# Float16 steps in pairs on TensorE, and the weights' float16 preparation at other slots

## The chip, the cores and the metric

One Trainium2 chip, one of its cores. The metric is the device time of one execution in microseconds, the median of several runs. A profile of a single execution, taken by the hardware profiler, stands beside the times.

## The reference

Two stages, in float32. First an attention through 32 inducing points, for 4 batches of 12416 rows of 128 values; then a gated feed-forward network (SwiGLU) over all 49664 rows.

```python
B, N, m, C = (4, 12416, 32, 128)          # x: (B, N, C), inducing: (m, C)
def mab(q, kv):
    s = scale * (q @ kv.transpose(0, 2, 1))
    s = s - s.max(-1, keepdims=True)
    a = np.exp(s)
    a /= a.sum(-1, keepdims=True) + 1e-09
    return a @ kv
h = mab(I, x)                             # 32 rows per batch
x = mab(x, h)                             # back to N rows
g = x @ w_gate                            # 128 -> 1536
silu = g * (1.0 / (1.0 + np.exp(-g)))
val = x @ w_val
return (silu * val) @ w_out               # 1536 -> 128
```

## The kernel before

The second attention is never multiplied out. Per batch, `tw` holds the 32 rows h projected through both weight matrices, and `stack` holds the attention weights of a tile of rows, transposed; one matmul of the two gives a 128 x 512 or 128 x 480 piece of g or of val. Both are split into a high and a low part so that float32r matmuls keep float32's accuracy.

A batch is 25 column tiles (`COLS`): one of 4 x 128 rows, twelve of 512, twelve of 480. A column tile has `NT` = 12 steps, t = 0 to 11, one for each 128 of the 1536 inner values. So a batch has 300 slots (`SLOTS`). In a slot, the main loop issues for one unit u:

- `front(u)`: two float32r matmuls on TensorE, g (line 787) and v (line 788), each into a buffer of the pool `ps_gv`, which has six.
- `gate(u)`: silu of g on ACT (line 793). It frees the g buffer.
- `value(u)`: the product of v and silu on DVE (line 801), into a buffer h, or, for t in `DVE_TILES` = {1, 5, 9} (`LAST_DVE` = {1, 7} in batch 3), in place in the v buffer.
- `split` of the unit before, which waited in the list `wait`: h_hi, the rounded product, by ACT (by DVE for t in `CAST`), line 814, and h_lo, the rest, by POOL, or by DVE for the units held in the v buffer, line 816. The unit then goes to the list `pend`.
- the attention's steps that are due at this slot, for this batch (`cur`) and the next (`nxt`).
- `back`: while `pend` and `wait` together hold more than `ahead` units, three matmuls of the oldest into o (lines 831, 832, 833: w_lo h_hi, w_hi h_hi, w_hi h_lo), in a buffer of the pool `ps_o`, which has two. After t = 11 DVE copies o to `ob` (line 841) and SP stores it.

From batch 0's column `CSW` = 13 on, and in all later batches, a unit is `half`: h_hi, h_lo and the weights of o are float16; g and v remain float32r. `ahead` is 5 (`SKEW`), grows by 1/6 a slot up to `HI` before a burst of exponentials (`bursts`, slots at which ACT computes the attention's exponentials), and falls back at it: TensorE then works off the stored units.

The schedule is manual: each engine executes its instructions in the order in which the program issues them, and waits only where data or a buffer require it. Steps of the attention carry a slot by hand (`plan`, `post`, `FIRST`). In batch 0 some more steps prepare float16: `peak_of` (nine reductions over the weights, line 190), `peak_a` and `peak_b` (their maximum over partitions through a matmul, line 198), `peak_c`, `peak_d`, the factors of h (`size_a` to `size_c`), `half_a` (w_hi + w_lo into `joint` on POOL, line 214), `half_b` and `half_c` (float16 weights, on ACT, line 218, and DVE, line 222), and `rise`, which scales val's part of `tw`. `acc` names the values of t at which a step that needs a `ps_o` buffer has to wait for a later slot.

Of the kernel before, what the change touches and what calls it, by code (L numbers as in the profile page):

```python
# [9 lines left out]
F32 = mybir.dt.float32  # L10
# [3 lines left out]
ALU = mybir.AluOpType  # L14
AX = mybir.AxisListType
# [4 lines left out]
P = 128  # L20
# [22 lines left out]
COLS = [(0, 0)] + [(q, j) for q in range(1, NF) for j in range(NG)]  # L43
SLOTS = len(COLS) * NT
NXT = 4
HI = 10
RAMP = 6
BF = (2, 3, 11, 10)
SKEW = 5
# [10 lines left out]
E0 = 36  # L60
TINY = 2.0 ** -50
LAST_DVE, LAST_CAST = {1, 7}, {5, 11}
WPK, WSZ, WOH, CSW = 104, 128, 134, 13

# [45 lines left out]
def induced_set_attention_then_swiglu(ctx: ExitStack, tc: tile.TileContext, xt, xn, ind, wgv, wo, out):  # L110
# [63 lines left out]
    nc.gpsimd.memset(wide, 2.0 ** 127)  # L174
    peak = const.tile([P, 12], F32, name="peak")
    top = const.tile([P, 36], F32, name="top")
    peaks = const.tile([P, P], F32, name="peaks")

    def floor2(out, in_):

        nc.vector.tensor_scalar(out=out.bitcast(U32), in0=in_.bitcast(U32), scalar1=0x7F800000, scalar2=None, op0=ALU.bitwise_and)
# [7 lines left out]
        at = 6 * k + i  # L189
        nc.vector.tensor_reduce(out=peak[:, at:at + 1], in_=w[:, WP * i:WP * i + WP], op=ALU.max, axis=AX.X, apply_absolute_value=True)  # L190

    def peak_a(k):
        nc.vector.tensor_reduce(out=peak[:, 10 + k:11 + k], in_=peak[:, (0, 6)[k]:(6, 9)[k]], op=ALU.max, axis=AX.X)
        nc.vector.tensor_scalar(out=peaks, in0=ones, scalar1=peak[:, 10 + k:11 + k], scalar2=None, op0=ALU.mult)

    def peak_b(k):
        ps = ps_gv.tile([P, 512], F32, name="gv")
        nc.tensor.matmul(out=ps[:, 0:P], lhsT=peaks, rhs=ident, start=True, stop=True)
        nc.vector.tensor_scalar(out=peaks, in0=ps[:, 0:P], scalar1=TINY, scalar2=None, op0=ALU.max, op1=ALU.max, accum_out=top[:, k:k + 1])

    def peak_c():
        floor2(top[:, 1:2], top[:, 1:2])
        inverse2(top[:, 2:3], top[:, 1:2])

# [65 lines left out]
    def attention(b, one, xn0=None, xt0=None):  # L270
# [180 lines left out]
            nc.vector.tensor_scalar(out=st.hV.bitcast(U32), in0=st.hT[:, 0:M].bitcast(U32), scalar1=0x7FFFFFFF, scalar2=None, op0=ALU.bitwise_and)  # L451

        def size_b():
            ps = ps_gv.tile([P, 512], F32, name="gv")
            nc.tensor.matmul(out=ps[:, 0:M], lhsT=ones, rhs=st.hV, start=True, stop=True)  # L455
            st.sc = att.tile([P, 8], F32, name="sc")
            c = lambda i: st.sc[:, i:i + 1]
            st.up, st.down = c(0), c(1)
            nc.vector.tensor_reduce(out=c(2), in_=ps[:, 0:M], op=ALU.max, axis=AX.X)
            nc.vector.tensor_scalar(out=c(3), in0=c(2), scalar1=top[:, 0:1], scalar2=TINY, op0=ALU.mult, op1=ALU.max)  # L460
            floor2(c(4), c(3))
            inverse2(c(5), c(4))
# [190 lines left out]
    def plan(st, p):  # L653

        f, s = st.f, []

        def add(slot, step, *args):
            def go():
                f[step](*args)


            go.acc = (NT - 1, 0, 1) + (2,) * (step == "hacc") if step in ("s1", "max_b", "hacc", "h_c", "s2") else ()
            s.append((slot, go))

        def blocks(q):
            return CH0[q], CH0[q] + CH[q]

        last = p["S1"][0] + p["S1"][1] * (NCH - 1)
        v1 = last - 3 * p["S1"][1]
        for q in range(NCH):  # L670
            add(p["LX"][0] + p["LX"][1] * q if q < NXT else v1 + 1 + 3 * (q - NXT), "load_xt", q)

            add(v1 if q < NXT else last, "s1", q, q not in (0, NXT))
        mb = last + p["MX"]
        add(last + 2, "max_a"), add(mb, "max_b")
        e1 = mb + p["E1"]
        for q in range(NXN):
            add(e1 - p["LN"][0] + p["LN"][1] * q, "load_xn", q)
            add(e1, "exp1_part", q)
            add(e1, "eT", q)  # L680
            add(e1 + p["HA"][q], "hacc", q, (0, NXN - 1))
        add(e1, "exp1_part", NXN, NCH - 1)
        for q in range(NXN, NCH):
            k = NXN + (q - NXN | 1)
            at = e1 + p["HB"][0] + p["HB"][1] * (k - NXN)
            add(max(at - p["HC"][0] - k + q, e1 + 1 + (p["HB"][0] + p["HB"][1] if q == NCH - 1 else p["HA"][0])), "load_xn", q)
            add(at - p["HC"][1] + 1 - k + q, "eT", q)
            add(at, "hacc", q, (k - 1, k))
        add(at, "h_a")
        add(at + 2, "h_b")  # L690
        hn = at + p["HD"]
        add(hn, "h_c")
        for i, step in enumerate(("size_a", "size_b", "size_c", "size_d")):
            add(hn + 3 * i + 2, step)
        for i, q in enumerate(S2O):
            k = i % NXT
            at = hn + 4 + p["H2"] * (NXT - 1) if i < NXT else hn + p["H2"] * (NCH - 1)
            add(at, "s2", *blocks(q), i not in (0, NXT))
# [162 lines left out]
    for b in range(B):  # L861
        nxt = attention(b + 1, (one, oneb)[(b + 1) % 2]) if b + 1 < B else None
        if nxt is not None:
            nxt.steps = plan(nxt, PA if b == 0 else PB)
            if b == 0:
                cur.steps.append((nxt.e1, lambda: run(f"e2:52:{NTB}")))
                for q in range(2, NF):
                    base = NT * (1 + NG * (q - 1) - NST) + 2
                    base = max(base, E0 + 4) if q < 4 else max(base, nxt.e1 + 1)
                    cur.steps += post(cur, q, nc.gpsimd, base)  # L870
                once = [lambda x=(k, i): peak_of(*x) for k in range(2) for i in range((6, 3)[k])]
                once += [lambda: cur.f["size_a"](), lambda: peak_a(0)]
                cur.steps += [(WPK + 2 * i, f) for i, f in enumerate(once)]
                once = [lambda: peak_b(0), lambda: peak_a(1), lambda: cur.f["size_b"](), lambda: peak_b(1), peak_c, peak_d, cur.f["size_c"]]
                cur.steps += [(WSZ + 2 * i, f) for i, f in enumerate(once)]
                cur.steps += [(WOH + 10 + 2 * i, lambda i=i: (half_a, half_b, half_c)[i // 3](i % 3)) for i in range(9)]
                cur.steps += [(NT * (CSW - 1) + 2 * i + 2, lambda i=i: cur.f["rise"](i)) for i in range(6)]
                cur.steps.sort(key=lambda x: x[0])
        bursts = (nxt.bursts if nxt is not None else set()) | ({E0} if b == 0 else set())
        last_burst = max(bursts, default=0)  # L880
        for slot in range(NT if b == 0 else 0, SLOTS):
            c, t = slot // NT, slot % NT
            u = front(cur, b, c, t)
            gate(u)
            value(u)
            u.cast_dve = t in (LAST_CAST if b == B - 1 else CAST)
            u.last = b == B - 1 and slot == SLOTS - 1
            if wait:
                split(wait[0])
                pend.append(wait.pop(0))  # L890
            wait.append(u)
            if slot in bursts:
                u.cast_dve = True
                split(u)
                pend.append(wait.pop(0))
            for a in (cur, nxt):
                while a is not None and a.steps and a.steps[0][0] <= slot:

                    if pend and pend[0].t in getattr(a.steps[0][1], "acc", ()):
                        break  # L900
                    a.steps.pop(0)[1]()
            ahead = min(ahead + 1 / RAMP, HI) if nxt is not None and slot < last_burst else max(ahead - 1 / RAMP, SKEW)
            if slot in bursts:
                ahead = SKEW - (b == 0)
            while len(pend) + len(wait) > ahead:
                back(pend.pop(0))
        if nxt is not None:
            nxt.steps = [(at - SLOTS, f) for at, f in nxt.steps]
        cur = nxt
# [41 lines left out]
```

## Time and profile before

| what | value |
|---|---|
| median of 3 runs | 1452.67 us (1452.27 to 1453.83) |
| the profiled execution | 1453.71 us |
| its span, first to last instruction | 1451.9 us |
| mean granted TensorE clock | 0.995 |
| busy share of the span | TensorE 99%, ACT 87%, DVE 83%, POOL 78% |
| batch 1's 300 slots | 349.5 us |
| batch 3, from its first slot | 331.2 us |

PE is TensorE's matmul, PEld its weight load, DVE VectorE, ACT ScalarE, POOL GpSimd, SP the engine that issues DMAs. A group's row gives line, engine, operation, output and inputs by the program's names, shapes and count, then busy us and mean ns of one, then idle time before it and who ended it. A timeline's row gives start and duration in us, then the same names, and in brackets the idle time before it with its releaser. A row of a stretch gives, for each engine, busy us and number of instructions, then the granted clock, the DMA engines' share and GB/s. The ends of matmuls are modelled and overlap, so it is their starts that tell the pace.

### The profile page before, as it was taken

Reading aid. Unit: us, or ns where it says so; the run is one execution under the profiler, and the core shown is the slowest. Engines: PE = TensorE matmul, PEld = TensorE weight load, DVE = VectorE, ACT = ScalarE, POOL = GpSimd, SP = SyncE. Lnnn points to the kernel's source line nnn. Section 1 sums busy time; section 2 is a strip of 40 time slices with the busy share of each in tenths; the row PEclk is TensorE's granted clock in tenths of the full one; section 3 lists DMA queues with packets and bytes.
Section 4 is the critical chain, followed back from the end, with each engine's and each line's share of the span. In section 5 each row is a group of like instructions: output and inputs, shape, how many; then the busy total and the mean of one; then the engine's idle time right before and its main releaser. Section 6 shows DMA issues by size and latency. Waiting matters only on the chain.

```text
span 1451.9 us, 25130 instructions
## 1 busy us (share of the span) xinstructions
PE 1434.0 (99%) x7512; PEld 825.1 (57%) x7512; DVE 1208.2 (83%) x2138; ACT 1266.5 (87%) x2366; POOL 1139.7 (78%) x1036
## 2 busy tenths in 40 slices
PE   9999998999999999999999999999999999999999
PEld 6577776555555555555555455455555555555554
DVE  6888878988888879888888878978888878888887
ACT  4889787789998788899999888799999898889897
POOL 1689768778788667787888767778878889889887
PEclk9999999999999999999999999999999999999999
DMA  9233522212132532121114324221111111111110
GB/s 373 63 98 119 180 87 85 96 52 76 32 111 76 185 129 106 52 70 41 42 36 144 129 88 137 106 74 49 39 42 43 32 42 45 31 44 39 41 42 21
DMA packets 50824, 119.82 MB, mean 83 GB/s; under 512 B 11392, under 2 KB 28288, under 8 KB 50688
## 3 DMA queue, kind: packets, MB, share of 16 engines
q1 hardware_dynamic: 50688, 118.22, 25.0%
q8 instruction: 59, 0.97, 0.3%
q14 instruction: 77, 0.63, 0.1%
HBM read 62.87 MB, written 25.43 MB: 61 GB/s over the span
## 4 chain that ended last, share of the span: by engine, by line
PE 81%; ACT 0%; DVE 0%; issue 0%; DVEq 0%
PE o L831 16%; PE gv L788 16%; PE gv L787 16%; PE o L833 15%; PE o L832 15%; PE gv L329 1%; PE o L377 1%; PE o L329 1%; PE gv L511 0%; ACT silu L793 0%; ACT h_hi L814 0%; DVE ob L841 0%; PE gv L390 0%; PE o L443 0%; PE gv L455 0%
## 5 line engine op out<-in xcount | busy, mean ns | idle before, releaser
L816 POOL TENSOR_TENSOR h_lo<-h,h_hi 128x480 f16<-128x480 f32 (+2 forms) x915 | 1035.4, 1153 | 262.8 <-ACT h_hi L814 185.3
L793 ACT ACTIVATE silu<-gv 128x512 f32<-128x512 f32 (+1 forms) x1200 | 702.8, 587 | 96.4 <-PE gv L787 73.5
L801 DVE TENSOR_TENSOR h<-gv,silu 128x512 f32<-128x512 f32 (+1 forms) x916 | 610.5, 668 | 185.0 <-ACT silu L793 126.3
L787 PE MATMUL gv<-stack,tw 128*128 128x512 f32 (+1 forms) x1200 | 654.1, 545 | 2.2 <-DVE h L801 1.0
L814 ACT CAST h_hi<-h 128x480 f16<-128x480 f32 (+2 forms) x788 | 475.2, 603 | 52.0 <-DVE h L801 45.8
L788 PE MATMUL gv<-stack,tw 128*128 128x512 f32 (+1 forms) x1200 | 466.6, 389 | 3.2 <-DVE h L801 2.3
L831 PE MATMUL o<-h_hi,wo_l 128*128 128x480 f16 (+1 forms) x1044 | 399.0, 382 | 0.0
L832 PE MATMUL o<-h_hi,wo_h 128*128 128x480 f16 (+1 forms) x1044 | 388.2, 372 | 0.0
L833 PE MATMUL o<-h_lo,wo_h 128*128 128x480 f16 (+1 forms) x1044 | 388.2, 372 | 0.0
L787 PEld LDWEIGHTS gv<-stack,tw 128*128 128x128 f32 x1200 | 227.7, 190 | 129.1 <-ACT tw L501 2.7
L831 PEld LDWEIGHTS <-wo_l 128*128 128x128 f16 x1044 | 100.3, 96 | 266.1 <-issue 260.9
L788 PEld LDWEIGHTS gv<-stack,tw 128*128 128x128 f32 x1200 | 227.7, 190 | 39.2 <-ACT silu L793 7.5
L801 DVE TENSOR_TENSOR gv<-gv,silu 128x512 f32<-128x512 f32 (+1 forms) x272 | 184.5, 678 | 30.7 <-ACT silu L793 28.8
L816 DVE TENSOR_TENSOR h_lo<-gv,h_hi 128x480 f16<-128x480 f32 (+2 forms) x272 | 181.0, 665 | 1.4
L833 PEld LDWEIGHTS <-wo_h 128*128 128x128 f16 x1044 | 102.2, 98 | 114.3
L814 ACT CAST h_hi<-gv 128x480 f16<-128x480 f32 (+2 forms) x269 | 153.0, 569 | 10.2 <-DVE gv L801 8.5
L832 PEld LDWEIGHTS <-wo_h 128*128 128x128 f16 x1044 | 104.8, 100 | 3.5
L841 DVE TENSOR_SCALAR ob<-o,sc 128x480 f32<-128x480 f32 (+1 forms) x87 | 62.9, 723 | 0.5 <-PE o L833 0.5
L814 DVE CAST h_hi<-h 128x480 f16<-128x480 f32 (+2 forms) x128 | 61.6, 482 | 0.0
L831 PE MATMUL o<-h_hi,wo_lo 128*128 128x512 f32 x144 | 57.8, 402 | 0.0
L832 PE MATMUL o<-h_hi,wo_hi 128*128 128x512 f32 x144 | 56.6, 393 | 0.0
L833 PE MATMUL o<-h_lo,wo_hi 128*128 128x512 f32 x144 | 56.4, 392 | 0.0
(194 smaller groups left out, 691.3 us busy)
## 6 DMA issues: line engine op xcount, KB each, us to landing
xt_sb<-xt SPq DMA_DIRECT2D x32, 896.0 KB, 5.1
xn_sb<-xn SPq DMA_DIRECT2D x18, 896.0 KB, 5.6
out<-ob SPq DMA_DIRECT2D x52, 256.0 KB, 2.0
out<-ob SPq DMA_DIRECT2D x48, 240.0 KB, 2.0
stack<-a_hi SPq DMA_DIRECT2D x96, 64.0 KB, 2.0
stack<-a_lo SPq DMA_DIRECT2D x96, 64.0 KB, 2.0
stack<-a_hi SPq DMA_DIRECT2D x96, 60.0 KB, 2.0
stack<-a_lo SPq DMA_DIRECT2D x96, 60.0 KB, 2.0
```

The lines of the kernel that those rows point to most:

```text
L329: nc.tensor.matmul(out=ps[32 * j:32 * j + 32, 32 * (lo - b0):32 * (hi - b0)], lhsT=lhsT, rhs=st.xt[q][:, lo - CH0[q]:hi - CH0[q], j, :], s ...
L377: nc.tensor.matmul(out=st.hps[32 * g:32 * g + 32, 0:C], lhsT=st.eT[q][:, 32 * i:32 * i + 32], rhs=st.xn[q][:, i, :], start=(tb < NG), stop ...
L787: nc.tensor.matmul(out=u.g[:, :n], lhsT=st.w[:, wcol(0, t)], rhs=rhs, start=True, stop=True)
L788: nc.tensor.matmul(out=u.v[:, :n], lhsT=st.w[:, wcol(1, t)], rhs=rhs, start=True, stop=True)
L793: nc.scalar.activation(out=u.s[:, :u.n], in_=u.g[:, :u.n], func=AF.Silu)
L801: nc.vector.tensor_mul(out=u.h[:, :n], in0=u.v[:, :n], in1=u.s[:, :n])
L814: (nc.vector.tensor_copy if u.cast_dve else nc.scalar.copy)(out=u.hi[:, :n], in_=u.h[:, :n])
L816: eng.tensor_sub(out=u.lo[:, :n], in0=u.h[:, :n], in1=back[:, :n])
L831: nc.tensor.matmul(out=o[:, :n], lhsT=w_lo[:, ws], rhs=u.hi[:, :n], start=(t == 0), stop=False)
L832: nc.tensor.matmul(out=o[:, :n], lhsT=w_hi[:, ws], rhs=u.hi[:, :n], start=False, stop=False)
L833: nc.tensor.matmul(out=o[:, :n], lhsT=w_hi[:, ws], rhs=u.lo[:, :n], start=False, stop=(t == NT - 1))
L841: nc.vector.tensor_scalar(out=ob[:, :n], in0=o[:, :n], scalar1=u.st.down, scalar2=None, op0=ALU.mult)
```

## The change

In float16 steps two slots are taken together. `front` is issued for both units (g v g v), then both silus, both products, then the splits, then the steps due at the two slots with the `back` of stored units between (at constant depth two units: six matmuls of o). `late` is the number of units left unsplit: one as before, or none where a burst falls into the pair or where the pair's second unit is held in its v buffer (t = 1, 5, 9; in batch 3 t = 1, 7). `HI` is 9 instead of 10. Float32 steps of batch 0 remain single.

In batch 0 the steps for float16 move: the nine `peak_of` from slots 104 to 120 to slots 56 to 72, `peak_a` and `peak_b` to 74 and 76, each now for both weight matrices at once, `peak_c` and `peak_d` to 78 and 80, the sizes from 122 to 140 to slots 82, 85, 88, and `half_a`, `half_b`, `half_c` from three, three, three at 144 to 160 to one piece after the other at 108 to 140, through one `joint` buffer instead of three. The matmuls of `peak_b` and `size_b` write to `ps_o` instead of `ps_gv`, and wait for a slot at which its second buffer is free.

```diff
-HI = 10
+HI = 9
-WPK, WSZ, WOH, CSW = 104, 128, 134, 13
+WPK, WOH, CSW = 56, 108, 13
...
-    def peak_a(k):
-        nc.vector.tensor_reduce(out=peak[:, 10 + k:11 + k], in_=peak[:, (0, 6)[k]:(6, 9)[k]], op=ALU.max, axis=AX.X)
-        nc.vector.tensor_scalar(out=peaks, in0=ones, scalar1=peak[:, 10 + k:11 + k], scalar2=None, op0=ALU.mult)
-
-    def peak_b(k):
-        ps = ps_gv.tile([P, 512], F32, name="gv")
-        nc.tensor.matmul(out=ps[:, 0:P], lhsT=peaks, rhs=ident, start=True, stop=True)
-        nc.vector.tensor_scalar(out=peaks, in0=ps[:, 0:P], scalar1=TINY, scalar2=None, op0=ALU.max, op1=ALU.max, accum_out=top[:, k:k + 1])
+    peaks = []
+
+    def peak_a():
+        peaks.append(eTp.tile([P, W], F32, name="eT"))
+        for k in range(2):
+            nc.vector.tensor_reduce(out=peak[:, 10 + k:11 + k], in_=peak[:, (0, 6)[k]:(6, 9)[k]], op=ALU.max, axis=AX.X)
+            nc.vector.tensor_scalar(out=peaks[0][:, P * k:P * k + P], in0=ones, scalar1=peak[:, 10 + k:11 + k], scalar2=None, op0=ALU.mult)
+
+    def peak_b():
+        ps = ps_o.tile([P, 512], F32, name="o")
+        for k in range(2):
+            nc.tensor.matmul(out=ps[:, P * k:P * k + P], lhsT=peaks[0][:, P * k:P * k + P], rhs=ident, start=True, stop=True)
+        nc.vector.tensor_reduce(out=top[:, 0:2], in_=ps[:, 0:2 * P].rearrange("p (k w) -> p k w", k=2), op=ALU.max, axis=AX.X)
...
-        joint[i] = sgl.tile([P, WP], F32, name="joint%d" % i)
+        joint[i] = sgl.tile([P, WP], F32, name="joint")
...
         def size_b():
-            ps = ps_gv.tile([P, 512], F32, name="gv")
+            ps = ps_o.tile([P, 512], F32, name="o")
...
-        for slot in range(NT if b == 0 else 0, SLOTS):
+        slot = NT if b == 0 else 0
+        while slot < SLOTS:
             c, t = slot // NT, slot % NT
-            u = front(cur, b, c, t)
-            gate(u)
-            value(u)
...
+            us = [front(cur, b, c, t)]
+            if us[0].half:
+                us.append(front(cur, b, c, t + 1))
+            slots = range(slot, slot + len(us))
+            slot += len(us)
+            for u in us:
...
+                gate(u)
+            for u in us:
+                value(u)
+            burst = any(x in bursts for x in slots)
+            if burst:
+                us[-1].cast_dve = True
+            late = 0 if burst or us[-1].on_dve and us[-1].half else 1
+            wait += us
+            while len(wait) > late:
                 split(wait[0])
                 pend.append(wait.pop(0))
...
+            for x in slots:
+                for a in (cur, nxt):
+                    while a is not None and a.steps and a.steps[0][0] <= x:
...
+                while len(pend) + len(wait) > ahead + (slots[-1] - x):
+                    back(pend.pop(0))
```

More of the change, by code (lines that the diff above doesn't have):

```diff
@@ L176, in induced_set_attention_then_swiglu @@
     top = const.tile([P, 36], F32, name="top")
-    peaks = const.tile([P, P], F32, name="peaks")
     def floor2(out, in_):
@@ L190, in peak_of @@
         nc.vector.tensor_reduce(out=peak[:, at:at + 1], in_=w[:, WP * i:WP * i + WP], op=ALU.max, axis=AX.X, apply_absolute_value=True)
-    def peak_a(k):
-        nc.vector.tensor_reduce(out=peak[:, 10 + k:11 + k], in_=peak[:, (0, 6)[k]:(6, 9)[k]], op=ALU.max, axis=AX.X)
-        nc.vector.tensor_scalar(out=peaks, in0=ones, scalar1=peak[:, 10 + k:11 + k], scalar2=None, op0=ALU.mult)
-    def peak_b(k):
-        ps = ps_gv.tile([P, 512], F32, name="gv")
-        nc.tensor.matmul(out=ps[:, 0:P], lhsT=peaks, rhs=ident, start=True, stop=True)
-        nc.vector.tensor_scalar(out=peaks, in0=ps[:, 0:P], scalar1=TINY, scalar2=None, op0=ALU.max, op1=ALU.max, accum_out=top[:, k:k + 1])
+    peaks = []
[9 more added lines that the diff above has]
+        nc.vector.tensor_reduce(out=top[:, 0:2], in_=ps[:, 0:2 * P].rearrange("p (k w) -> p k w", k=2), op=ALU.max, axis=AX.X)
     def peak_c():
+        nc.vector.tensor_scalar(out=top[:, 1:2], in0=top[:, 1:2], scalar1=TINY, scalar2=None, op0=ALU.max)
         floor2(top[:, 1:2], top[:, 1:2])
@@ L659, in go @@
                 f[step](*args)
-            go.acc = (NT - 1, 0, 1) + (2,) * (step == "hacc") if step in ("s1", "max_b", "hacc", "h_c", "s2") else ()
+            go.acc = (NT - 1, 0, 1) + (2,) * (step == "hacc") if step in ("s1", "max_b", "hacc", "h_c", "s2", "size_b") else ()
             s.append((slot, go))
@@ L871, in induced_set_attention_then_swiglu @@
                 once = [lambda x=(k, i): peak_of(*x) for k in range(2) for i in range((6, 3)[k])]
-                once += [lambda: cur.f["size_a"](), lambda: peak_a(0)]
+                once += [peak_a, peak_b, peak_c, peak_d]
+                peak_b.acc = (NT - 1, 0, 1)
                 cur.steps += [(WPK + 2 * i, f) for i, f in enumerate(once)]
-                once = [lambda: peak_b(0), lambda: peak_a(1), lambda: cur.f["size_b"](), lambda: peak_b(1), peak_c, peak_d, cur.f["size_c"]]
-                cur.steps += [(WSZ + 2 * i, f) for i, f in enumerate(once)]
-                cur.steps += [(WOH + 10 + 2 * i, lambda i=i: (half_a, half_b, half_c)[i // 3](i % 3)) for i in range(9)]
+                size = [cur.f[f"size_{k}"] for k in "abc"]
+                size[1].acc = (NT - 1, 0, 1)
+                cur.steps += [(WPK + 2 * len(once) + 3 * i, f) for i, f in enumerate(size)]
                 cur.steps += [(NT * (CSW - 1) + 2 * i + 2, lambda i=i: cur.f["rise"](i)) for i in range(6)]
+                cur.steps += [(WOH + 4 * i, lambda i=i: (half_a, half_b, half_c)[i % 3](i // 3)) for i in range(9)]
                 cur.steps.sort(key=lambda x: x[0])
@@ L880, in induced_set_attention_then_swiglu @@
         last_burst = max(bursts, default=0)
-        for slot in range(NT if b == 0 else 0, SLOTS):
+        slot = NT if b == 0 else 0
+        while slot < SLOTS:
             c, t = slot // NT, slot % NT
-            u = front(cur, b, c, t)
-            gate(u)
-            value(u)
-            u.cast_dve = t in (LAST_CAST if b == B - 1 else CAST)
-            u.last = b == B - 1 and slot == SLOTS - 1
-            if wait:
+            us = [front(cur, b, c, t)]
[4 more added lines that the diff above has]
+            for u in us:
+                u.cast_dve = u.t in (LAST_CAST if b == B - 1 else CAST)
+                u.last = b == B - 1 and u is us[-1] and slot == SLOTS
+                gate(u)
[7 more added lines that the diff above has]
+            while len(wait) > late:
@@ L889, in induced_set_attention_then_swiglu @@
                 split(wait[0])
                 pend.append(wait.pop(0))
[L891 to L906, printed above, removed]
+            for x in slots:
+                for a in (cur, nxt):
+                    while a is not None and a.steps and a.steps[0][0] <= x:
+                        if pend and pend[0].t in getattr(a.steps[0][1], "acc", ()):
+                            break
+                        a.steps.pop(0)[1]()
+                ahead = min(ahead + 1 / RAMP, HI) if nxt is not None and x < last_burst else max(ahead - 1 / RAMP, SKEW)
+                if x in bursts:
+                    ahead = SKEW - (b == 0)
+                while len(pend) + len(wait) > ahead + (slots[-1] - x):
+                    back(pend.pop(0))
```

## The prediction

> **What bounds the kernel now.** I read the page first, then the stretches of the four batches, then TensorE's and the other engines' timelines in one steady column.
>
> ```profile
> span 1451.9 us, 25130 instructions
> PE 1434.0 (99%) x7512; PEld 825.1 (57%) x7512; DVE 1208.2 (83%) x2138; ACT 1266.5 (87%) x2366; POOL 1139.7 (78%) x1036
> ```
>
> ```profile
> core 0: us, PE busy (x) PEld busy (x) DVE busy (x) ACT busy (x) POOL busy (x), PEclk, DMA share, GB/s
> 249.30:417.80 168.50, 165.83 (x826) 93.98 (x826) 145.55 (x263) 146.45 (x279) 135.34 (x128) 0.99 0.22 67
> 417.80:767.30 349.50, 349.37 (x1849) 189.26 (x1847) 295.22 (x522) 313.66 (x588) 271.63 (x247) 1.00 0.27 86
> 1116.80:1448.00 331.20, 331.20 (x1516) 179.21 (x1514) 272.16 (x454) 295.68 (x551) 290.75 (x261) 1.00 0.13 38
> ```
>
> The three stretches are batch 0's float16 part, batch 1 (batch 2 has the same schedule) and batch 3. TensorE is never idle in the last two, so a step takes what its five matmuls take. ACT is busy 90%, DVE 84% of batch 1: there is some slack, but it is slack of queues that serve one unit at a time.
>
> **What pairing is worth on TensorE.** Columns of a timeline row: start in us, duration, engine, line, tiles.
>
> ```profile
> 423.66 0.40 PE L788 MATMUL gv<-stack,tw 128*128 128x512 f32 x1
> 424.12 0.39 PE L788 MATMUL gv<-stack,tw 128*128 128x512 f32 x1
> 424.82 0.58 PE L787 MATMUL gv<-stack,tw 128*128 128x512 f32 x1
> 429.34 0.58 PE L787 MATMUL gv<-stack,tw 128*128 128x512 f32 x1
> 513.60 0.39 PE L831 MATMUL o<-h_hi,wo_l 128*128 128x512 f16 x1
> 517.28 0.38 PE L833 MATMUL o<-h_lo,wo_h 128*128 128x512 f16 x1
> 1100.61 0.56 PE L787 MATMUL gv<-stack,tw 128*128 128x480 f32 x1
> 1109.09 0.56 PE L787 MATMUL gv<-stack,tw 128*128 128x480 f32 x1
> ```
>
> From 424.82 to 429.34 lie four steps of 512 columns: 4.52/4 = 1.13 us. From 1100.61 to 1109.09 lie eight of 480: 1.06 us. The trace already holds both halves of the new order. Where the backlog grows, two g v follow each other: v to v 0.46 us for two float32 matmuls. At 513.60 six units of o run in a row: 17 starts in 3.68 us, 0.2165 each. A pair is then one step with one change each way, and two more float32 and three more float16 matmuls: 1.13 + 0.46 + 0.65 = 2.24 us against 2.26. That is 0.02 a pair; rounding of the rows leaves 0.01 to 0.03. The weight loads at the type change look dear in the groups but nearly all of them lies under streaming. 1044 float16 steps are 522 pairs: 10 us (5 to 15), if nothing else ends later than TensorE.
>
> **What pairing adds elsewhere.** This is the part that I let decide. Before, unit u's cast stands on ACT behind silu of u+1, and its subtraction on DVE (t = 1, 5, 9) behind the product of u+1: each has a step's time to become ready. Now a pair whose second unit is one of those splits both units at once (late = 0). DVE's order becomes product, product, subtraction, and the subtraction waits for a cast that waits for the second product. Behind it on DVE stand the column's copy to ob, the attention's steps and the next pair's products. On ACT that cast stands ahead of the next pair's two silus. In the other pairs the first unit's cast (which waits for its product of the same pair) stands ahead of the next silus, and DVE's next product waits for them. DVE and ACT hand work to each other in a ring. Prices, from a steady column of 480:
>
> ```profile
> 1097.71 0.70 DVE L841 TENSOR_SCALAR ob<-o,sc 128x480 f32<-128x480 f32 x1
> 1098.34 0.66 DVE L801 TENSOR_TENSOR gv<-gv,silu 128x480 f32<-128x480 f32 x1
> 1099.84 0.65 DVE L816 TENSOR_TENSOR h_lo<-gv,h_hi 128x480 f16<-128x480 f32 x1
> 1100.40 0.65 DVE L801 TENSOR_TENSOR h<-gv,silu 128x480 f32<-128x480 f32 x1
> 1101.58 0.56 ACT L793 ACTIVATE silu<-gv 128x480 f32<-128x480 f32 x1
> 1101.59 0.62 DVE L801 TENSOR_TENSOR h<-gv,silu 128x480 f32<-128x480 f32 x1
> 1102.18 0.67 DVE L801 TENSOR_TENSOR gv<-gv,silu 128x480 f32<-128x480 f32 x1
> 1102.24 0.59 ACT L814 CAST h_hi<-h 128x480 f16<-128x480 f32 x1
> 1102.74 0.56 ACT L793 ACTIVATE silu<-gv 128x480 f32<-128x480 f32 x1
> 1102.75 0.67 DVE L566 TENSOR_REDUCE a_hi<-aT 128x512 fp32r<-128x512 f32 x1
> 1103.20 0.55 ACT L814 CAST h_hi<-gv 128x480 f16<-128x480 f32 x1
> ```
>
> Start to start, a product holds DVE 0.58 (0.59 and 0.57), a subtraction 0.56, the copy to ob 0.63, a cast ACT 0.50. A handover takes 0.03: the product of 1101.59 ends at 1102.21, its cast starts at 1102.24; the silu of 1101.58 ends at 1102.14 and the product starts at 1102.18.
>
> A pair with a DVE unit, from its first product to the next pair's: 0.58 until the second product, 0.67 for it, 0.03, cast 0.55, 0.03, subtraction 0.56 = 2.42 us. A pair without: product 0.65, 0.03, cast 0.50, silu 0.56, 0.04 = 1.78. They alternate; at depth 5 the copy to ob falls into the pair t = 4, 5 behind its subtraction and adds 0.63. A column of 480 needs 3 x 4.20 + 0.63 = 13.23 us. TensorE took 12 x 1.06 = 12.72 and would take 12.60. So the ring, not TensorE, sets the column, 0.51 us slower than before.
>
> ```profile
> L793 ACT ACTIVATE silu<-gv 128x512 f32<-128x512 f32 x624 | 373.6, 600 | 59.5 <-PE gv L787 46.4 <-DVE h L801 3.3 <-DVE h_hi L801 0.7
> L801 DVE TENSOR_TENSOR h<-gv,silu 128x512 f32<-128x512 f32 x472 | 321.4, 684 | 96.2 <-ACT silu L793 56.8 <-POOL h_lo L816 12.1 <-issue 9.4
> L801 DVE TENSOR_TENSOR gv<-gv,silu 128x512 f32<-128x512 f32 x140 | 97.2, 695 | 20.7 <-ACT silu L793 19.3 <-PE gv L788 0.8
> L814 ACT CAST h_hi<-gv 128x512 f16<-128x512 f32 x102 | 59.3, 581 | 4.8 <-DVE gv L801 4.1
> ```
>
> At 512, with 0.03 more for each start to start: 0.61 + 0.70 + 0.03 + 0.58 + 0.03 + 0.60 = 2.55 and 0.68 + 0.03 + 0.53 + 0.60 + 0.04 = 1.88; a column 3 x 4.43 + 0.66 = 13.95 against 12 x 1.13 = 13.56: 0.39 slower. The six gv buffers hold three units, so TensorE can run ahead of the ring by little more than 1 us before its matmul waits for a silu; a lag of 0.5 a column is used up in about two columns.
>
> Batch 1 has 12 columns of 480 and 13 of 512: 12 x 0.51 + 13 x 0.39 = 11.2 us. Its other work: TensorE did 349.5 - 12 x 12.72 - 13 x 13.56 = 20.6 us beside the steps.
>
> ```profile
> 515.35 1.28 ACT L361 ACT_TABLE_LOAD   x1
> 520.47 1.28 ACT L793 ACT_TABLE_LOAD   x1
> ```
>
> The ring pays instead for what stands in it: the first burst of exponentials keeps ACT 6.4 us (515.35 to 521.75), the second has the same two table loads, and DVE's attention and post steps are up to 295.2 less about 250 for the columns (12 products, 3 subtractions, a cast of some 0.4 and the copy: 9.7 us at 480, 10.2 at 512), some 40 us. Against that, 75 pairs without a DVE unit leave DVE 0.6 us idle each (1.78 less two products), 45 us of room. Bounds for the difference to TensorE's 20.6: 0 and +30. I take +7, nearer the low end, because the room is as large as the steps. So 18 us for each of batches 1 and 2, and 6 for batch 0's twelve columns of 480. In batch 3 the DVE units are t = 1, 7: two dear pairs and four of 1.78 make 11.96, below 12.60, so TensorE bounds it and it gains 150 x 0.02 = 3 us.
>
> **The weights' steps in batch 0.**
>
> ```profile
> 203.00:216.00 13.00, 10.03 (x111) 8.22 (x110) 6.46 (x14) 9.32 (x18) 4.01 (x4) 0.87 0.41 141
> 208.55 0.49 PE L198 MATMUL gv<-ident,peaks 128*128 128x128 f32 x2 [2.97 <-ACT silu L793]
> 208.97 4.15 PE L377 MATMUL o<-xn_sb,eT 128*32 128x128 f32 x84
> 520.32 2.60 PE L377 MATMUL o<-xn_sb,eT 128*32 128x128 f32 x84
> 246.21 0.69 DVE L801 TENSOR_TENSOR h<-gv,silu 128x512 f32<-128x512 f32 x1 [1.77 <-POOL h_lo L816]
> 111.00:130.00 19.00, 18.77 (x82) 14.72 (x81) 16.30 (x27) 17.24 (x33) 18.39 (x17) 1.00 0.61 194
> L190 DVE TENSOR_REDUCE peak<-wgv_sb x6: 669/676/677, 174.3 to 188.1; 128x1 f32<-128x512 f32 x6
> ```
>
> The bound's matmul needed a gv buffer whose silu stood behind the exponentials: 2.97 us of idle TensorE, and the 84 matmuls behind it took 4.15 instead of 2.60 at a granted clock of 0.87. It moves from slot 128 to 76 and into ps_o, ahead of any burst. Three sums of the weights leave POOL's crowded slots 144 to 148 for 108, 120, 132; the waits of DVE for POOL there (1.77 the longest) mostly go. Worth up to 2.97 + 1.55 + 1.8 = 6.3. Added: nine reductions of 0.68, 0.6 of DVE each (5.5 us), now come into 111 to 130 us, where DVE has 2.7 idle: up to 2.8. The matmul waits at its new slot for peak_a two slots earlier, under 1 us. I take -3.5 (bounds -6.3 and +3). The sizes, half_b, half_c and the single joint buffer (its next sum waits for half_c four slots back, 4.5 us) cost nothing visible: each instruction is there as before. No DMA is added; those of attention steps move by one slot at most on SP, under leads of many slots. HI at 9 takes one banked o, 0.65 us, from each of five bursts; the pair gives ACT one silu before the burst instead, so I count nothing.
>
> **Sum.** 2 x 18 + 6 - 3 - 3.5 = +35.5 on the profiled execution's 1453.71 us, which lies 1.0 above the median of 1452.67. So 1488 on the median's scale.
>
> **Rivals.** (A) TensorE stays the bound: -10 - 3.5, 1439 us. It holds if the ring has over 5% more speed than I worked out (13.23 to 12.60 at 480). For it: no queue bounds anything now. Against: each link is a quoted duration, and both engines issue in program order in every row. (B) The ring binds in the columns alone and the other work hides: 2 x 11.2 + 6 - 6.5 = +22, 1475. (C) The bursts also let TensorE idle so long that its clock falls as at 203 to 216: 1.55 us at five bursts, +8, 1496. The Trainium skill, TensorE: Matmul & The Clock Gate, section What's actually happening, states half the clock after an idle window of about 3.4 us; the 2.97 and 0.87 above agree, and by that rule short waits in each pair would cost no clock. (D) The type change costs the same per pair as before and the ring is hidden: -3.5 alone, 1449.
>
> **Chances.** Forecast 0.45, B 0.15, C 0.10: slower together 0.70. A 0.24. D 0.06, whose 0.24% lies at the edge of 0.2%, about what a measurement of this kernel can tell from no change: half of it counts as faster, half as same. The forecast's own range is 1470 to 1506; the one asked for reaches to A's upper half, 1440.
>
> **What would show it.** Right: the longest new wait is DVE's h_lo for ACT's h_hi in the same pair, TensorE's g or v waits for silu a little in nearly every pair of batches 0 to 2, TensorE's share falls to about 97%, columns of 13.2 and 13.9 us there but about 12.6 and 13.45 in batch 3; no 3 us gap at the bound's matmul. Wrong: columns of 12.6 us in batch 1, and no wait of h_lo for h_hi on DVE.

## The result, and the profile after

The changed kernel takes 1540.86 us in the median (1540.01 to 1542.47), the one before 1453.25 on the same chip: a ratio of 1.0604 [1.0588, 1.062]. The forecast was 1488, with a range of 1440 to 1506. The sign and the place were right; the amount was not: +88 us where +35.5 were worked out.

The profiled execution took 1540.01 us. The head of its page:

```profile
span 1538.2 us, 25195 instructions
PE 1492.5 (97%) x7512; PEld 856.9 (56%) x7512; DVE 1215.5 (79%) x2133; ACT 1246.5 (81%) x2369; POOL 1138.1 (74%) x1036
```

DVE and ACT have the work that they had (1208.2 and 1266.5 us before); only their shares fell. The count of each engine's instructions is nearly the same, so what was added is waiting. The stretches (batch 0 from slot 12 to 155, batch 0 from 156, batches 1, 2, and 3 to the end of the span; columns as in the prediction's stretches):

```profile
56.00:252.80 196.80, 187.35 (x1027) 140.21 (x1025) 167.07 (x287) 160.40 (x294) 155.90 (x129) 0.99 0.34 112
252.80:432.60 179.80, 173.65 (x825) 97.25 (x826) 140.77 (x256) 143.30 (x278) 132.59 (x127) 1.00 0.20 61
432.60:813.40 380.80, 370.63 (x1848) 199.03 (x1847) 295.21 (x520) 309.64 (x589) 271.74 (x248) 1.00 0.25 79
813.40:1193.60 380.20, 370.64 (x1848) 198.97 (x1847) 295.58 (x520) 309.69 (x589) 271.70 (x248) 1.00 0.24 78
1193.60:1538.20 344.60, 338.80 (x1517) 189.24 (x1515) 276.15 (x456) 286.25 (x554) 291.52 (x263) 1.00 0.12 37
```

Batch 1 went from 349.3 to 380.8 us at a granted clock of 1.00. (PE counts 370.63 us busy where it counted 349.37 before, for the same matmuls of the same shapes: part of the waiting is counted as busy, and the figure is no sign of more work.) The table counts each stretch from the first g matmul of its first slot, against the prediction's sum:

| stretch | before, us | after, us | difference | forecast |
|---|---|---|---|---|
| up to slot 155 | 249.3 | 252.8 | +3.5 | -3.5 |
| batch 0 from slot 156 | 168.5 | 179.9 | +11.4 | +6 |
| batch 1 | 349.3 | 380.8 | +31.5 | +18 |
| batch 2 | 349.4 | 380.2 | +30.8 | +18 |
| batch 3, to the end | 335.4 | 344.6 | +9.2 | -3 |
| span | 1451.9 | 1538.2 | +86.3 | +35.5 |

The first row holds the start-up, which no edit touches: up to slot 12 it took 56.9 us before, 55.5 after, and 55.5 to 57.0 in the profiles of all the runs below, so 1 or 2 us of that row are chance. From slot 12 to 155 alone the change costs +4.9 us (192.4 before, 197.3 after).

The list of waits of the changed kernel (total us, times, longest; its first four rows and the seventh):

```profile
POOL h_lo L821 <- ACT h_hi L819: 240.3, 300, 7.5
ACT h_hi L819 <- DVE h L806: 211.6, 373, 2.6
DVE h_lo L821 <- ACT h_hi L819: 119.5, 211, 1.0
PEld gv L793 <- ACT silu L798: 87.2, 254, 1.1
DVE h L806 <- POOL h_lo L821: 63.9, 107, 1.3
```

The third row is the new one: DVE's subtraction waits for ACT's cast 211 times, 0.57 us each. The fourth is what TensorE pays for it, in 254 places: v waits for a buffer whose silu is late. And in the second row, from the other side, ACT's cast waits for DVE's product: 45.8 us before, 211.6 now. Two engines that wait for each other are a ring, and a steady column of 480 shows its links. DVE first (start, duration, line, tiles, idle before; a cast and three short operations of the attention are left out):

```profile
773.82 0.66 DVE L806 TENSOR_TENSOR h<-gv,silu 128x480 f32<-128x480 f32 x1 [0.62 <-issue]
774.39 0.66 DVE L806 TENSOR_TENSOR gv<-gv,silu 128x480 f32<-128x480 f32 x1
775.73 0.66 DVE L821 TENSOR_TENSOR h_lo<-gv,h_hi 128x480 f16<-128x480 f32 x1 [0.37 <-ACT h_hi L819]
776.30 1.21 DVE L806 TENSOR_TENSOR h<-gv,silu 128x480 f32<-128x480 f32 x2
778.14 0.66 DVE L806 TENSOR_TENSOR h<-gv,silu 128x480 f32<-128x480 f32 x1
778.71 0.66 DVE L806 TENSOR_TENSOR gv<-gv,silu 128x480 f32<-128x480 f32 x1
780.05 0.66 DVE L821 TENSOR_TENSOR h_lo<-gv,h_hi 128x480 f16<-128x480 f32 x1 [0.68 <-ACT h_hi L819]
780.62 0.71 DVE L846 TENSOR_SCALAR ob<-o,sc 128x480 f32<-128x480 f32 x1
781.25 1.21 DVE L806 TENSOR_TENSOR h<-gv,silu 128x480 f32<-128x480 f32 x2
```

and ACT in the same stretch:

```profile
776.99 0.59 ACT L819 CAST h_hi<-h 128x480 f16<-128x480 f32 x1 [0.35 <-DVE h L806]
777.48 1.02 ACT L798 ACTIVATE silu<-gv 128x480 f32<-128x480 f32 x2
778.40 1.08 ACT L819 CAST h_hi<-h 128x480 f16<-128x480 f32 x2
779.46 0.56 ACT L819 CAST h_hi<-gv 128x480 f16<-128x480 f32 x1
779.91 1.04 ACT L798 ACTIVATE silu<-gv 128x480 f32<-128x480 f32 x2
```

Read the pair of 778.14: its second product, in place in the v buffer, ends at 778.71 + 0.66 = 779.37, its cast starts at 779.46 and ends at 780.02, the subtraction starts at 780.05. DVE stood idle for 0.68 us, and behind it stood the copy and the next products. From first product to first product, a pair with a DVE unit takes 773.82 to 776.30 = 2.48 us, with the copy 778.14 to 781.25 = 3.11, a pair without 776.30 to 778.14 = 1.84. So a column takes 3 x (2.48 + 1.84) + 0.63 = 13.59 us; columns without other work measure 13.6. TensorE, the first g matmul of three pairs:

```profile
773.74 0.55 PE L792 MATMUL gv<-stack,tw 128*128 128x480 f32 x1
775.83 0.56 PE L792 MATMUL gv<-stack,tw 128*128 128x480 f32 x1
778.06 0.56 PE L792 MATMUL gv<-stack,tw 128*128 128x480 f32 x1
```

The first pair, in which it waits for nothing, takes 2.09 us, 0.03 less than two single steps of 1.06; the next, with a wait for a silu in it, takes 2.23.

### The profile page after: what moved, and what is told of

Same layout as the page of the kernel before. It is cut to its first block, busy times and chain, and to the rows that moved or that the text cites. A ratio compares the mean times of both kernels' runs of the same rounds, so it can differ in the third digit from the quotient of the medians.

```text
span 1538.2 us, 25195 instructions
## 1 busy us (share of the span) xinstructions
PE 1492.5 (97%) x7512; PEld 856.9 (56%) x7512; DVE 1215.5 (79%) x2133; ACT 1246.5 (81%) x2369; POOL 1138.1 (74%) x1036
## 5 line engine op out<-in xcount | busy, mean ns | idle before, releaser
L806 DVE TENSOR_TENSOR h<-gv,silu 128x512 f32<-128x512 f32 (+1 forms) x916 | 591.7, 667 | 166.1 <-POOL h_lo L821 63.9
L798 ACT ACTIVATE silu<-gv 128x512 f32<-128x512 f32 (+1 forms) x1200 | 646.5, 586 | 33.9 <-PE gv L792 31.9
L819 ACT CAST h_hi<-h 128x480 f16<-128x480 f32 (+2 forms) x791 | 464.9, 608 | 215.1 <-DVE h L806 211.6
L792 PE MATMUL gv<-stack,tw 128*128 128x512 f32 (+1 forms) x1200 | 570.7, 476 | 9.5 <-ACT silu L798 4.1
L793 PE MATMUL gv<-stack,tw 128*128 128x512 f32 (+1 forms) x1200 | 493.2, 411 | 10.2 <-ACT silu L798 7.0
L836 PE MATMUL o<-h_hi,wo_l 128*128 128x480 f16 (+1 forms) x1044 | 393.8, 377 | 0.9 <-DVE hn L402 0.9
L821 DVE TENSOR_TENSOR h_lo<-gv,h_hi 128x480 f16<-128x480 f32 (+2 forms) x272 | 183.1, 673 | 121.2 <-ACT h_hi L819 119.5
L819 DVE CAST h_hi<-h 128x480 f16<-128x480 f32 (+2 forms) x125 | 68.2, 547 | 0.1
```

The source lines that it names most:

```text
L792: nc.tensor.matmul(out=u.g[:, :n], lhsT=st.w[:, wcol(0, t)], rhs=rhs, start=True, stop=True)
L793: nc.tensor.matmul(out=u.v[:, :n], lhsT=st.w[:, wcol(1, t)], rhs=rhs, start=True, stop=True)
L798: nc.scalar.activation(out=u.s[:, :u.n], in_=u.g[:, :u.n], func=AF.Silu)
L806: nc.vector.tensor_mul(out=u.h[:, :n], in0=u.v[:, :n], in1=u.s[:, :n])
L819: (nc.vector.tensor_copy if u.cast_dve else nc.scalar.copy)(out=u.hi[:, :n], in_=u.h[:, :n])
L821: eng.tensor_sub(out=u.lo[:, :n], in0=u.h[:, :n], in1=back[:, :n])
```

## The experiments

Each edit is made in the changed kernel or in the kernel before, as its text says; a ratio is always to the kernel before. Theory 1 is that of the prediction, the ring of DVE and ACT; the rivals were the h buffers, the weights' steps and the pairing as such.

**Only the rule on `late` undone.** In the changed kernel, the pair with a DVE unit keeps its second unit for the next pair like any other:

```diff
-            late = 0 if burst or us[-1].on_dve and us[-1].half else 1
+            late = 0 if burst else 1
```

> Of the paired kernel one line: late is 1 except at a burst, so the DVE-held second unit is split one pair later, its cast behind the next pair's silus. Theory 1, the ring (DVE's subtraction waits for a cast of its own pair, and that cast stands ahead of the next silus): every pair then costs the ring 1.8 to 1.9 us, six of them 11.3, below TensorE's 12.6, so columns of 480 in batch 1 fall from 13.6 to 12.6-12.8, the wait of h_lo on DVE for h_hi (119.5 us) falls below 20, and the kernel takes 1470 to 1490 us. Theory 2, the three h buffers (a pair takes two at once, POOL still reads the third): the product's waits for POOL's h_lo stay or grow, columns stay above 13.3, over 1520 us.

1452.92 us, 0.9992 [0.9983, 1.0001]: all 88 us are back, more than was expected of this line. Batch 1, and the wait of v for silu:

```profile
418.00:766.40 348.40, 347.79 (x1849) 199.27 (x1847) 294.81 (x521) 304.88 (x588) 271.08 (x248) 1.00 0.27 87
```

```profile
PEld gv L793 <- ACT silu L798: 8.2, 26, 0.8
```

TensorE is busy 347.79 of 348.40 us, as before. ACT and then DVE in a steady stretch of it:

```profile
773.36 1.10 ACT L798 ACTIVATE silu<-gv 128x512 f32<-128x512 f32 x2
774.33 0.60 ACT L819 CAST h_hi<-gv 128x512 f16<-128x512 f32 x1
```

```profile
774.06 1.29 DVE L806 TENSOR_TENSOR h<-gv,silu 128x512 f32<-128x512 f32 x2
775.27 0.68 DVE L821 TENSOR_TENSOR h_lo<-gv,h_hi 128x512 f16<-128x512 f32 x1
```

The cast of the unit held in v now follows the next pair's silus, and the subtraction the next pair's products: the cast ended at 774.93, 0.34 us before DVE comes to it. The plain pairs' in-pair casts, the other half of the ring as forecast, are in this kernel too, and cost nothing that shows: columns of 480 take 12.6 us. But here, save after a burst, the cast of an older unit stands ahead of them, which gives the product time; after the change a plain pair follows an emptied list, and its first cast has nothing to work on while it waits. Batch 3 is back too, with the three h buffers of the change (335.4 us before, 344.6 after):

```profile
1115.10:1449.90 334.80, 329.91 (x1517) 190.61 (x1515) 272.62 (x455) 286.92 (x551) 288.73 (x262) 1.00 0.13 38
```

**Four h buffers instead of three** in the changed kernel:

```diff
-BF = (2, 3, 11, 10)
+BF = (2, 4, 11, 10)
```

> Of the paired kernel one number: four h buffers instead of three. Theory 1 (ring): columns of 480 in batches 1 and 2 stay at 13.5-13.6; only batch 3, where the ring has no part, may gain its 9 us, so 1525 to 1541 us. Theory 2 (h buffers): the 64 us of product waits for POOL go, columns in batch 1 fall below 13.1, under 1505 us.

1533.19 us, 1.0552 [1.0535, 1.0568]. Batches 1 and 2 do not move (380.8 and 381.0). Batch 3 does, from 344.6 to 337.1:

```profile
430.80:811.60 380.80, 370.97 (x1849) 198.94 (x1847) 295.27 (x520) 309.57 (x589) 272.11 (x248) 1.00 0.25 79
1192.60:1529.70 337.10, 331.43 (x1517) 190.73 (x1515) 269.85 (x456) 287.66 (x554) 292.42 (x263) 1.00 0.13 38
```

DVE's waits in batch 3, of the changed kernel and then of this one:

```profile
DVE h L806 <- POOL h_lo L821: 41.8, 66, 0.8
```

```profile
DVE h L806 <- POOL h_lo L821: 10.7, 19, 0.9
```

A pair without a DVE unit takes two h buffers at once, and with three its product waits for POOL's subtraction of the pair before. In batches 1 and 2, where the ring binds, a fourth buffer gains nothing; in batch 3, with a third fewer DVE units, it gains 7.5 us. The three buffers do not make that loss by themselves, though: with `late` at 1 batch 3 took 334.8 us with three, and products waited 20.2 us for POOL there. It takes the early split and the three buffers together.

**The weights' steps alone**, in the kernel before (their new slots, the single `joint`, the matmuls into `ps_o`; single steps, `HI` 10):

```diff
-WPK, WSZ, WOH, CSW = 104, 128, 134, 13
+WPK, WOH, CSW = 56, 108, 13
...
```

> The kernel before, with only the weights' steps at their new slots (single steps, HI 10). The stretch up to slot 156 in the paired kernel was 3.5 us longer than before, with TensorE waiting 2.75 us for peak_a at the moved bound's matmul. If that wait is the moved steps' own, this kernel is 2 to 5 us slower than before (1455 to 1458). The prediction's step would have it 3.5 us faster (1449.5).

1452.49 us, 0.9999 [0.999, 1.0008]: nothing, and so neither of the two outcomes named. From slot 12 on it is 6.9 us behind the kernel before at slot 80 and 1.8 at slot 156; in the rest of batch 0 it is 0.8 faster. The gap at the bound's matmul was moved, not removed. TensorE in the changed kernel, first the bound's matmul, then the stretches before it and from it on:

```profile
138.72 1.23 PE L202 MATMUL o<-ident,eT 128*128 128x128 f32 x4 [2.75 <-DVE eT L197]
```

```profile
134.00:138.60 4.60, 1.97 (x9) 1.31 (x7) 4.41 (x11) 3.25 (x7) 3.83 (x3) 1.00 0.01 2
138.60:142.30 3.70, 3.58 (x11) 3.06 (x12) 2.04 (x7) 1.18 (x3) 1.92 (x2) 0.54 0.02 4
```

It now waits 2.75 us for DVE, which is busy 4.41 of the 4.60 us before it: with a cast, the last of the nine reductions, two products, a subtraction and a reduction of the attention, and only from 137.67 on with `peak_a`. Then TensorE runs 3.7 us at a granted clock of 0.54.

**The pairs alone**, in the kernel before, with `late` as in the change and `HI` 9:

```diff
+            late = 0 if burst or us[-1].on_dve and us[-1].half else 1
...
```

> The kernel before, with only the paired loop and HI 9, the weights' steps at their old slots. If the two parts add, it stands 2 to 5 us below the paired kernel: 1535 to 1540 us. If the weights' steps at the new slots were needed for the pairs (or the pairs' loss came from them), it differs by more than 10 us either way.

1539.0 us, 1.0587 [1.0573, 1.0602], with batch 1 at 380.2: the whole loss, to 2 us. From slot 12 to 155, where it differs from the kernel before in `HI` alone, it takes 192.1 us, before 192.4.

**Both units split in their own slot, in every pair** of the changed kernel:

```diff
-            late = 0 if burst or us[-1].on_dve and us[-1].half else 1
+            late = 0 if burst or us[-1].half else 1
```

> Of the paired kernel one line: every pair splits both units at once (late 0 in all pairs), not only those with a DVE-held unit. The suspected cost doubled on ACT alone: in the other pairs no subtraction stands on DVE, but the second cast now waits for its product ahead of the next silus. The ring: 1.25 to the end of the second product, 0.09, cast 0.50, silu 0.57, 0.09 = 2.5 us in each of the six pairs, columns of 480 at 15 (against 13.6), the kernel near 1600 us. If it is DVE's wait for the cast alone that costs, columns stay at 13.6 to 13.9 and the kernel below 1555 us.

1624.24 us, 1.1183 [1.1162, 1.1203]; columns of 480 take 14.7 us. Taking the late split from the other three pairs as well doubles the loss. Two of them take 2.40 us where they took 1.84; the third, t = 10 and 11, stays at 1.83, and its second unit is the one whose cast DVE does (`CAST` = {11}). So 3 x 2.48 + 2 x 2.40 + 1.83 + 0.63 = 14.70: what slows a plain pair is ACT's cast ahead of the next silus, with no subtraction on DVE in it. ACT's cast now waits for DVE's product 267.8 us and DVE's subtraction for the cast 160.2 (211.6 and 119.5 after the change).

**The cast of the DVE units on DVE**, so that the early split would need no handover:

```diff
-                u.cast_dve = u.t in (LAST_CAST if b == B - 1 else CAST)
+                u.cast_dve = u.t in (LAST_CAST if b == B - 1 else CAST) or u.on_dve and u.half
```

> Of the paired kernel one line: the DVE-held units' cast is done by DVE, just ahead of its subtraction; the units are still split in their own pair. The way over ACT is gone. The ring: a pair with such a unit 0.57 + 0.57 + cast 0.4 + 0.56 = 2.1 us, a pair without 1.85, with the copy to ob 0.63: 12.5 a column, at TensorE's 12.6. Theory ring: columns of 480 at 12.6 to 12.9 and 1455 to 1475 us. If the early split costs by something else (buffers freed in another order, POOL served in bursts), it stays above 1515 us.

1589.83 us, 1.0945 [1.093, 1.096]: worse than the change, and the expectation failed. DVE:

```profile
801.75 0.66 DVE L806 TENSOR_TENSOR h<-gv,silu 128x480 f32<-128x480 f32 x1 [0.35 <-ACT silu L798]
802.32 0.66 DVE L806 TENSOR_TENSOR gv<-gv,silu 128x480 f32<-128x480 f32 x1
803.01 0.66 DVE L819 CAST h_hi<-gv 128x480 f16<-128x480 f32 x1
803.71 0.66 DVE L821 TENSOR_TENSOR h_lo<-gv,h_hi 128x480 f16<-128x480 f32 x1
```

I had priced the cast at the 0.40 of a cast from h. From the v buffer it takes 0.66, and the cast and the subtraction each start 0.69 to 0.70 after the operation that they depend on, where independent ones follow at 0.57. The pair's four take 801.75 to 804.28, 2.53 us against 2.48 with ACT's cast in between. DVE is now busy where it used to wait, 344.10 us of batch 1 instead of 295.21, so the attention's steps find less room too.

**DVE units first in their pair** (t = 0, 4, 8; in batch 3 0, 6). The rule on `late` asks for the second unit and so never applies:

```diff
-DVE_TILES = {1, 5, 9}
+DVE_TILES = {0, 4, 8}
...
-LAST_DVE, LAST_CAST = {1, 7}, {5, 11}
+LAST_DVE, LAST_CAST = {0, 6}, {5, 11}
```

> Of the paired kernel the tiles held by DVE only: t = 0, 4, 8 (0, 6 in batch 3), the first of their pair, so late is 1 there; their cast still follows their product within the pair, but the pair's other product stands between. The ring: 0.65 + 0.03 + cast 0.55 + 0.03 + subtraction 0.56 = 1.83 us in those pairs, 1.85 in the others, 11.1 + 0.63 a column, below TensorE's 12.6: columns 12.6 to 12.8, 1450 to 1465 us. If same-pair splits of DVE's units cost as such, 1500 or more.

1452.19 us, 0.9997 [0.9988, 1.0007], columns of 12.6. The subtraction is in the same pair as its product, as after the change, but a product stands between them in which the cast can run: DVE's wait of h_lo for h_hi is 18.6 us in all, 99 times, instead of 119.5. Batch 3 takes 333.9 us with three h buffers, though products wait 38.8 us for POOL in it: such waits need not cost anything.

**The early split in single steps.** In the kernel before, with no pairs, a unit held in the v buffer is split in its own slot:

```diff
             if slot in bursts:
                 u.cast_dve = True
+            if slot in bursts or u.on_dve and u.half:
                 split(u)
                 pend.append(wait.pop(0))
```

> The kernel before, single steps, with only the early split: a DVE-held unit is split in its own slot. DVE then waits for the cast as in the pairs (product 0.66, 0.09, cast 0.55, 0.03, subtraction 0.56: 1.9 us until the next product), but only one unit in four, and the three products behind it can follow at 0.6 to 0.9 each: 1.9 + 3 x 0.75 = 4.15 us against 4.24 for TensorE's four steps. Theory ring: TensorE stays the bound, 1450 to 1462 us; the loss needs the pair's second product and the two silus behind the cast. If an early split costs by itself, over 1480 us.

1586.6 us, 1.0917 [1.0902, 1.0931]: 133 us slower with no pair in it, where next to nothing was expected. So the pairing is not what costs. DVE and then ACT:

```profile
774.98 1.21 DVE L801 TENSOR_TENSOR h<-gv,silu 128x480 f32<-128x480 f32 x2
776.82 0.66 DVE L801 TENSOR_TENSOR h<-gv,silu 128x480 f32<-128x480 f32 x1 [0.62 <-issue]
777.39 0.40 DVE L814 CAST h_hi<-h 128x480 f16<-128x480 f32 x1
777.71 0.66 DVE L801 TENSOR_TENSOR gv<-gv,silu 128x480 f32<-128x480 f32 x1
779.05 0.66 DVE L816 TENSOR_TENSOR h_lo<-gv,h_hi 128x480 f16<-128x480 f32 x1 [0.68 <-ACT h_hi L814]
779.62 1.21 DVE L801 TENSOR_TENSOR h<-gv,silu 128x480 f32<-128x480 f32 x2
```

```profile
775.66 0.59 ACT L814 CAST h_hi<-h 128x480 f16<-128x480 f32 x1 [0.35 <-DVE h L801]
776.16 1.03 ACT L793 ACTIVATE silu<-gv 128x480 f32<-128x480 f32 x2
777.51 0.59 ACT L814 CAST h_hi<-h 128x480 f16<-128x480 f32 x1 [0.32 <-DVE h L801]
778.45 0.56 ACT L814 CAST h_hi<-gv 128x480 f16<-128x480 f32 x1 [0.35 <-DVE gv L801]
```

The chain of four units can be read off start by start: product 774.98, cast 775.66, silu 776.16, product 776.82, DVE's cast 777.39, product 777.71, cast 778.45, subtraction 779.05, next product 779.62. That is 4.64 us, and TensorE's four steps are 4.24; with the copy to ob, columns take 14.2. I had thought that the subtraction's 0.68 us would be made up by the three products behind it. They can't: the early split also empties the list of units that wait, so the next cast (775.66) has no older unit to work on and waits for its own slot's product, and the silu behind it comes late as well. Every four units start the same chain again. In the paired order the chain over four units is 2.48 + 1.84 = 4.32, which is why the change loses less than this.

**Late split, four h buffers, and the bound's matmul six slots behind its maxima**, in the changed kernel:

```diff
-BF = (2, 3, 11, 10)
+BF = (2, 4, 11, 10)
...
-                cur.steps += [(WPK + 2 * i, f) for i, f in enumerate(once)]
+                cur.steps += [(WPK + 2 * i + 4 * (i > 9), f) for i, f in enumerate(once)]
...
-            late = 0 if burst or us[-1].on_dve and us[-1].half else 1
+            late = 0 if burst else 1
```

> Three edits of the paired kernel: late 1 except at bursts, four h buffers, and peak_b six slots behind peak_a instead of two (what follows it four slots later). Late 1 alone took 1452.9 us, with 197.1 us in batch 0 up to slot 156 against 192.4 before. If the wait for peak_a at the bound's matmul (2.75 us) and the slow clock behind it make those 5 us, and four buffers free what products wait for POOL, 1444 to 1449 us, faster than before by 0.3 to 0.6%. If TensorE's pairs give nothing, 1452 to 1454.

1448.35 us, 0.9971 [0.9961, 0.9982]. The number lies in the range that was expected, but half of the reason given for it failed: the gain is in the float16 stretches alone (batch 1 takes 347.3), and from slot 12 to 155 it takes 198.6 us, no less than the 197.1 with `late` alone. The group of the attention's matmuls into `ps_o` shows that the wait moved once more, to the next user of the buffer, out of which the bound's maximum had not yet been read:

```profile
L334 PE MATMUL o<-xt_sb,indT 128*32 128x448 f32 x48 | 5.8, 551 | 2.2 <-DVE top L203 2.2
```

**Late split, four h buffers, and the weights' bound and sizes at the slots of before** (the pieces of the float16 weights one after the other through one `joint`, three slots apart from slot 140), in the changed kernel:

```diff
-BF = (2, 3, 11, 10)
+BF = (2, 4, 11, 10)
...
-WPK, WOH, CSW = 56, 108, 13
+WPK, WSZ, WOH, CSW = 104, 128, 134, 13
...
+                cur.steps += [(WOH + 6 + 3 * i, lambda i=i: (half_a, half_b, half_c)[i % 3](i // 3)) for i in range(9)]
...
-            late = 0 if burst or us[-1].on_dve and us[-1].half else 1
+            late = 0 if burst else 1
```

> The paired loop with late 1 except at bursts and four h buffers, with the bound and sizes at their old slots (104, 128) and the three weight pieces one after the other through one joint buffer, at slots 140 to 164. With the old slots batch 0 up to slot 156 took 192.1 us in the pairs-only kernel against 198.6 in the kernel with late 1, four buffers and new slots, 1448.4 us. If that is all the moved steps' doing, 1441 to 1445 us, faster than before by 0.6 to 0.8%; if the late pieces hold up the first float16 columns, 1446 to 1452.

1446.35 us, 0.996 [0.9947, 0.9974]: 0.4% faster than the kernel before, and in the second of the two ranges expected, that of late pieces. From slot 12 to 155 it gains 2.2 us on before (no run tells the fourth buffer from the new order of the pieces there); batches 1, 2 and 3 gain 1.6, 1.8 and 1.3; the rest of batch 0 is 0.7 slower, its first float16 column 19.5 us long (17.1 before), while the last pieces of the weights are still being prepared.

## Why the prediction was half right

**What bounds.** Right: the order of DVE and ACT, not TensorE, sets the float16 stretches. Most marks named for it are there: the wait of h_lo for h_hi on DVE, v's wait for silu (in 254 places, fewer than "nearly every pair"), TensorE's share of 97%. The columns were longer than named, in batch 3 too, and the gap at the bound's matmul was still there. Rivals A and D (TensorE stays the bound) fall with columns of 13.6 instead of 12.6, B (columns alone) with the table, and C with a granted clock of 1.00 in every float16 stretch, some 250 short waits notwithstanding.

**The pair on TensorE.** Right in the row: 2.09 against 2.12, with 0.02 forecast; and with the ring gone a column of 480 without other work takes 12.60 instead of 12.72. But even then a batch gains 1.3 to 1.8 us (the last kernel above), not the 3 of 150 pairs. In its batch 1 the twelve columns of 480 gain 1.4 and the thirteen of 512, among which the attention's work stands, 0.3. Where the rest goes (the bursts with `HI` at 9 are one candidate) no run separates.

**Ring, first term mis-sized: the handover.** I took 0.03 to 0.04 us for each. That holds from a product in h to its cast and from a cast to its subtraction. From the product in the v buffer to its cast it is 0.09 (779.37 to 779.46), and from a silu to its product 0.09 too, as rows of the kernel before show (1106.57 + 0.57 = 1107.14 to 1107.23):

```profile
1106.57 0.57 ACT L793 ACTIVATE silu<-gv 128x480 f32<-128x480 f32 x1
1107.23 0.66 DVE L801 TENSOR_TENSOR h<-gv,silu 128x480 f32<-128x480 f32 x1 [0.41 <-ACT silu L793]
```

The row that I had read 0.04 from, the product of 1102.18, starts 0.59 behind another product: DVE itself can have held it, and it does not measure the handover. Two pairs take 4.32 instead of 4.20, a column of 480 13.59 instead of 13.23. At 512 the most frequent lengths in batches 1 and 2 are 2.61 and 1.92 instead of 2.55 and 1.88, 0.30 a column. Over 36 columns of 480 and 26 of 512 that is 13 + 8 = 21 us of the 51 that were missed; for 512 it is an estimate, as no column of 512 there is free of other work.

**Ring, second term: the other work.** Taken at +7 a batch beside the columns, between 0 and +30. Batches 1 and 2 lost 31 each; the columns as measured account for 12 x 0.87 + 13 x 0.69 = 19.4, which leaves about 12: some 5 too few, twice. A likely reason is that a step in the 0.6 us of room of a plain pair delays the products for which ACT waits; no run separates it.

**Batch 3: the step that failed outright.** I compared the ring's 11.96 with TensorE's 12.60 and stopped. With the measured handovers the ring is still below (2 x 2.48 + 4 x 1.84 = 12.32), and with a fourth h buffer columns without other work do take 12.60. Left out was that a plain pair takes two of the three h buffers at once, and that a ring of 12.32 leaves little room for a wait for POOL: +9.2 instead of -3. A fourth buffer returns 7.5 of it, and the late split returns all of it with three (334.8), so both are needed for the loss. The sum had no term for these buffers; the profile before shows products waiting 12.1 us for POOL's h_lo in one group alone.

**The weights' steps.** Forecast -3.5, with "under 1 us" for the wait at the new slot. It is 2.75, with 3.7 us at about half clock behind it, and alone the steps are worth nothing (0.9999; from slot 12 to 155, 194.2 against 192.4 before). I had the cost of the nine reductions and the wait for `peak_a` as two numbers; they belong together, since the last reduction and the products stand ahead of `peak_a` on a DVE that is busy 4.41 of 4.60 us. The Trainium skill, TensorE: Matmul & The Clock Gate, section What's actually happening, gives an idle window of about 3.4 us for the half clock. Here 2.75 us were followed by a granted clock of 0.54, within 4.6 us in which TensorE was busy 1.97, so an idle time below that figure is no guarantee. The 2.97 us of the kernel before, which the prediction counted as agreeing, lie below it as well.

**HI, the sizes, the single joint.** Counted as nothing. The weights' run, with the single `joint` and the sizes moved, bears that out for these two. `HI` has no run of its own, but up to slot 155 two pairs of kernels differ in nothing else. With the weights' steps at their old slots, 9 instead of 10 changes nothing (192.4 before, 192.1 in the pairs alone, from slot 12); at the new slots it costs 3.1 us (194.2 in the weights alone, 197.3 after the change), all of it between slots 120 and 132. So of the +4.9 there, 1.8 come with the steps alone and 3.1 more with `HI` at 9 on top of them; why it costs only there stays open.

**The terms together.** Of the 51 us missed, 21 are the handovers, some 9 the other work of batches 1 and 2, 12 batch 3, 7 the stretch up to slot 155 (start-up included) and 1 the rest of batch 0.

**What I had not seen: which half of the ring closes it.** The prediction has two kinds of pair, both slowed by in-pair casts. With `late` at 1 throughout, the plain pairs split their first unit as before, behind an older unit's cast, and nothing is lost; the single steps with the early split lose more than the pairs do. So the pairing is innocent, and one condition on one line makes the regression, down to batch 3 with its three buffers: where a split is moved from behind the next unit's work to ahead of it, and the list of waiting units is emptied by it, the one thing that the two queues had to hide each other's latency is gone.

## What to carry to other kernels

When two engines hand a unit back and forth, count the units that stand between a result and its use in each queue; at zero, the engines' busy shares (81% and 79% here) say nothing, and the period is the sum of the links from start to start, with the measured handovers. A change that issues two units at once takes their buffers two at a time: go through each pool that the units pass, and ask whether the engine that waits for one has time to spare; the same three h buffers cost 7.5 us in batch 3 with the early split and nothing without it. Before a loss is put down to the main idea of a change, run the kernel before with each of its side conditions alone.

## What the runs showed of the hardware

A handover between DVE and ACT was not one number: 0.03 us from a product in h to its cast and from a cast to its subtraction, 0.09 from a product in the v buffer to its cast and from a silu to its product. On DVE itself an operation that needed the one just before started 0.69 to 0.70 us after it, an independent one 0.57 (128 x 480, the product, cast and subtraction of a unit in the v buffer). DVE's cast to float16 took 0.66 us from the v buffer and 0.40 from h.
